# GpSimd's share of the expert chain in halves behind the diagonal, and four kinds of work placed later

## The chip, the cores and the metric

The kernel runs on one core of one Trainium2 chip. The metric is the device time of one execution in microseconds (us). Three runs of the kernel before took 696.67, 700.36 and 705.64 us; the median is 700.36 us. The profiled execution took 699.89 us, of which the profile shows a span of 698.1 us.

## The reference

Four batches of 11456 tokens go through an attention with 49 agents, and the result through a mixture of eight experts of which each token takes one.

```python
def _attn_ref(q, k, v, agents):            # q, k, v: 4 x 11456 x 128, agents: 4 x 49 x 128
    a2k = sm(agents, k)                    # softmax over the tokens
    agent_v = a2k @ v                      # 4 x 49 x 128
    q2a = sm(q, agents)                    # softmax over the 49 agents
    return q2a @ agent_v

def _moe_ref(x, expert_emb, tau, w1, w2):  # x: 45824 x 128, w1: 8 x 128 x 1024, w2: 8 x 1024 x 128
    logits = normed(x) @ normed(expert_emb).T / tau
    expert_idx = argmax(logits); gate_w = softmax(logits)[expert_idx]
    for e in range(8):
        out[mask_e] = gate_w * (relu(x[mask_e] @ w1[e]) @ w2[e])
```

All is float32.

## The kernel before

Per batch `b` the kernel runs over units `u` of eight tokens per partition (and a rest unit): scores of the agents with the keys (`k1_f32`, `k1_pairs`), the product with the values (`k2_unit`), the scores of the queries (`q_unit`), and the expert network over tiles `t` of four tokens per partition (`ffn_mm1`, `ffn_mm2`, `ffn_out`). It assumes that nearly all tokens of a batch take one expert, and prepares that expert's two weight matrices so that only 256 of the 1024 hidden columns have to be worked out for each token; the rest is a linear map (`lin`). Each token is then tested (`proved`, the `vp` products) on whether this was allowed, and the few tokens that fail are marked (`mark_strays`) and done again one by one: `fix(b)` for those of the batch's own expert, `stray` for those of another.

While batch b's network runs, keys, values and queries of batch b+1 are worked through, and near the end of batch b comes what is called **the chain** below: `pick_expert(b+1)`. It loads the expert (`load_expert`: w1s, w2s, one buffer each), forms `gp` = w1 times agent values, from that a sort key for each of the 1024 columns (eight a partition, tiles `mean`, `pw`, `key`: a dozen tiny VectorE instructions, lines 755 to 775), spreads the keys along a diagonal (`diag`, in the tile `sel`, line 772), turns them into one row by a product with ones (`row`, line 784), ranks each column against the row (lines 793 and 795), makes a selection matrix from the ranks (`sel`, line 801), and places the chosen columns (`placed`: gh and gl, the halves of w1; line 809). Then come `linp` (line 842), `w2pp` and its copy `w2p` (lines 856 and 858), the maximum over all partitions that gives the thresholds (`allmax`: a transpose `mT`, a VectorE maximum `mTx`, a product `mB`), a second selection (line 875) and a third `placed`, from which `vm`, the matrix of the tests, is made (line 880). The network of batch b+1 can begin with gh and gl (`hp`, line 1211), its second half needs `w2p` and `lin` (`yp`, lines 1235 to 1249), its tests need `vm`. The chain comes once in the opening (batch 0) and three times under a running network: 0 to 1, 1 to 2 and 2 to 3.

In the chain GpSimd (POOL) has four large instructions: w2s times its scale (line 735) and the remainder of w2 (line 736), the remainder of the placed columns gt (line 790), and diag (line 772, on GpSimd for b > 0).

What sets the order: every engine works through its own list in order. Python generators yield "steps" and so bring the pieces of all stages into one sequence; from that a scheduler makes the list of every engine when the kernel is built, except that the DMA queue of SyncE (SP) keeps the written order. `in_place(y_last)` ties a TensorE instruction behind the last product of the network. Tiles rotate through a few buffers: PSUM has four for `hp`, `fTp` and `vp`, two for `yp` and two for all else (`pss`); a TensorE instruction waits until the engine that reads the old content is done. The transposes of the queries' scores (`tt`, DMA, line 935) go through SP's queue as the key, value, query and expert loads do.

## Time and profile before

| what | value |
|---|---|
| median of three runs | 700.36 us (696.67 to 705.64) |
| profiled execution | 699.89 us, span 698.1 us |
| TensorE busy | 652.2 us, 93% |
| VectorE busy | 535.5 us, 77% |
| ScalarE busy | 453.6 us, 65% |
| GpSimd busy | 355.1 us, 51% |
| mean granted TensorE clock | 0.969 of full speed |

TensorE's two clock levels are 1.2 and 2.4 GHz; the granted clock of a stretch is its mean as a share of the higher. A wait in a view of the trace is idle time of an engine just before an instruction, with the instruction that ended it. An engine that is held up inside an instruction counts as busy: its instruction only lasts longer than others of its form.

### The profile page before, as it was taken

How to read it: one execution, taken by the hardware profiler on the slowest of the kernel's cores; microseconds unless marked ns; L12 is line 12 of the kernel's file. 1: busy time of each engine (PE TensorE's matmuls, PEld its weight loads, DVE VectorE, ACT ScalarE, POOL GpSimd, SP SyncE). 2: the span in 40 equal slices, each digit the busy share in tenths (PEclk: the TensorE clock that was granted, in tenths of full speed). 3: DMA queues.
4: the chain of work that ended last, by engine and by line, in shares of the span. 5: the costliest groups of instructions: out<-in, count | busy, mean ns of one | idle time of the engine just before them, and what ended most of it. 6: DMA issues, size and time to landing. Idle time of an engine off the chain costs nothing. (4 is left out here: it accounts for less than half of the span.)

```text
span 698.1 us, 23174 instructions
## 1 busy us (share of the span) xinstructions
PE 652.2 (93%) x9227; PEld 557.9 (80%) x9227; DVE 535.5 (77%) x1470; ACT 453.6 (65%) x1127; POOL 355.1 (51%) x606
## 2 busy tenths in 40 slices
PE   8998999999998888989999888999999999996996
PEld 6886888888887767878889677888888798775876
DVE  5767796878686988876767888977657889985983
ACT  3538746966887636847688853776577857992632
POOL 6002382675153745873533484685645656876410
PEclk9999999999999989989999997999999999998999
DMA  8995596699692267996959245998575424205141
GB/s 342 281 341 174 133 287 169 144 277 238 204 252 69 62 173 194 303 255 160 256 147 221 83 106 136 267 279 204 151 170 169 113 65 114 59 17 171 54 147 70
DMA packets 157047, 123.16 MB, mean 176 GB/s; under 512 B 76787, under 2 KB 133191, under 8 KB 156939
## 3 DMA queue, kind: packets, MB, share of 16 engines
q1 hardware_dynamic: 143499, 97.97, 55.5%
q10 hardware_dynamic: 13120, 23.47, 9.7%
q8 instruction: 73, 1.20, 0.7%
q14 instruction: 35, 0.29, 0.1%
q0 software_dynamic: 320, 0.24, 0.1%
HBM read 80.26 MB, written 23.79 MB: 149 GB/s over the span
## 5 line engine op out<-in xcount | busy, mean ns | idle before, releaser
L1065 ACT ACTIVATE vp<-vp 128x512 f32<-128x512 f32 x180 | 106.1, 590 | 18.7 <-PE vp L1056 13.1
L1220 ACT ACTIVATE hh<-hp 128x512 f16<-128x512 f32 (+1 forms) x124 | 72.4, 591 | 51.7 <-PE hp L1212 30.7
L438 PE MATMUL sp<-aT_all,fT 128*64 128x49 f32 x2496 | 96.4, 226 | 3.4 <-DVE avx L543 2.0
L1221 DVE SCALAR_TENSOR_TENSOR hh<-hp,hh 128x512 f16<-128x512 f32 (+1 forms) x124 | 82.9, 674 | 21.1 <-ACT hh L1220 18.6
L438 PEld LDWEIGHTS sp<-aT_all,fT 128*64 128x64 f32 x2496 | 84.3, 139 | 16.3 <-issue 3.6
L1247 PE MATMUL yp<-w2p,hh 128*128 128x128 f16 (+1 forms) x492 | 95.0, 223 | 0.1
L1248 PE MATMUL yp<-w2p,hh 128*128 128x128 f16 (+1 forms) x492 | 94.9, 223 | 0.0
L1249 PE MATMUL yp<-w2p,hh 128*128 128x128 f16 (+1 forms) x492 | 93.7, 223 | 0.0
L1056 PE MATMUL vp<-vm,tt 128*128 128x256 f16 x360 | 71.0, 274 | 3.9 <-DVE vmin L1062 2.3
L931 POOL TENSOR_TENSOR e<-qe,e 128x392 f16<-128x392 f32 (+1 forms) x48 | 42.2, 880 | 63.3 <-ACT e L928 62.2
L1211 PE MATMUL hp<-tt,gh 128*128 128x512 f16 (+1 forms) x184 | 69.5, 378 | 3.9 <-DVE hh L1221 1.6
L1263 DVE TENSOR_TENSOR ot<-yp,gs 128x512 f32<-128x512 f32 (+1 forms) x92 | 61.2, 668 | 14.6 <-PE yp L1244 8.7
L430 ACT COPY fT<-fTp 128x512 f32<-128x512 f32 (+1 forms) x103 | 57.0, 569 | 23.6 <-PE fTp L425 19.7
L1006 POOL TENSOR_TENSOR nrm<-qq,half 128x16 f32<-128x16 f32 (+2 forms) x28 | 69.9, 2498 | 0.2
L1212 PE MATMUL hp<-tt,gl 128*128 128x512 f16 (+1 forms) x184 | 69.3, 377 | 0.0
L1235 PE MATMUL yp<-lin,tt 128*128 128x128 f16 x720 | 64.9, 224 | 4.5 <-DVE ot L1263 4.4
L1244 PE MATMUL yp<-w2f,hh 128*128 128x128 f32 (+1 forms) x456 | 66.3, 283 | 0.0
L1244 PEld LDWEIGHTS yp<-w2f,hh 128*128 128x128 f32 (+1 forms) x456 | 60.0, 195 | 4.3 <-issue 0.8
L1235 PEld LDWEIGHTS <-tt 128*128 128x128 f16 x720 | 51.1, 102 | 12.3 <-issue 6.0
L425 PE MATMUL fTp<-ident,qt 128*128 128x128 f32 x360 | 55.0, 284 | 1.2 <-ACT hh L1216 0.9
L1247 PEld LDWEIGHTS <-hh 128*128 128x128 f16 (+1 forms) x492 | 49.4, 100 | 4.4 <-ACT hh L1220 0.3
L963 POOL TENSOR_TENSOR rt<-qe 128x392 f32<-128x392 f32 (+1 forms) x48 | 38.4, 800 | 28.2 <-ACT qe L923 20.1
(371 smaller groups left out, 1713.3 us busy)
## 6 DMA issues: line engine op xcount, KB each, us to landing
kt<-in_k_dram SPq DMA_DIRECT2D x44, 512.0 KB, 5.9
vt<-in_v_dram SPq DMA_DIRECT2D x44, 512.0 KB, 7.3
qt<-in_q_dram SPq DMA_DIRECT2D x44, 512.0 KB, 5.2
out_dram<-ot ACTq DMA_DIRECT2D x88, 256.0 KB, 2.3
w1s<-in_moe_w_dram SPq DMA_DIRECT2D x9, 512.0 KB, 5.2
w2s<-in_moe_w_dram SPq DMA_DIRECT2D x9, 512.0 KB
tt<-e SPq DMA_TRANSPOSE x48, 5.2
kt<-in_k_dram SPq DMA_DIRECT2D x4, 96.0 KB, 3.8
```

Of the source, the lines that this page charges most:

```text
L438: pe.matmul(out=s[h : h + w, c * A : (c + 1) * A], lhsT=xT[:, c * p + h : c * p + h + w], rhs=aT_all[:, b, :], start=True, stop=True, skip ...
L1006: pool.tensor_tensor(out=nrm, in0=quad, in1=half[:, :n], op=ALU.pow)
L1056: pe.matmul(out=z[:p, i * FP : (i + 1) * FP], lhsT=tt[:, c * p : (c + 1) * p], rhs=bt.vm[:, LO:], start=True, stop=True)
L1065: act.activation(z[:p], z[:p], AF.Relu, scale=-1.0, accum_out=bt.vsum[:p, at : at + 1])
L1211: pe.matmul(out=hp[:, :m], lhsT=bt.gh[:, fs], rhs=tt, start=True, stop=False)
L1220: h_last[:] = [act.activation(hh[:, :m], hp[:, :m], AF.Relu)]
L1221: dve.scalar_tensor_tensor(out=hl[:, :m], in0=hp[:, :m], scalar=0.0, in1=hh[:, :m], op0=ALU.max, op1=ALU.subtract)
L1235: pe.matmul(out=yp[:p, c, :], lhsT=tc_, rhs=bt.lin[:, h], start=(c == 0 and h == 0), stop=False, skip_group_check=True)
L1244: y_last[:] = [pe.matmul(out=y, lhsT=hh[:, cs], rhs=bt.w2f[:, f], start=False, stop=last, skip_group_check=True)]
L1247: pe.matmul(out=y, lhsT=hh[:, cs], rhs=wh, start=False, stop=False, skip_group_check=True)
L1248: pe.matmul(out=y, lhsT=hh[:, cs], rhs=wl, start=False, stop=False, skip_group_check=True)
L1249: y_last[:] = [pe.matmul(out=y, lhsT=hl[:, cs], rhs=wh, start=False, stop=last, skip_group_check=True)]
```

## The change

Six things change, all for the chains under a running network (b > 0) if nothing else is said.

- GpSimd's four large instructions are cut into halves, and those of w2s, w2x and gt are tied behind the second half of the diagonal. The two tiny VectorE instructions `nkey` and `sgn` move ahead of the diagonal.
- The VectorE remainder of a key unit (`ks`) is written in two instructions of four tokens instead of one of eight.
- The copy of `w2pp` to `w2p` goes from VectorE to ScalarE.
- The threshold products `mT` and `mB` are asked for some steps later and tied behind the network's last product.
- `mark_strays(b)` goes on when the next batch's `vm` exists, not when its `w2p` does.
- In `fix`, the token gather is asked for first, and for b < 3 the expert load 24 steps after it.

```diff
@@ -208,15 +208,18 @@
             except StopIteration as s:
                 return s.value
 
-    def allmax(col, n, tag, psx, g, bufs=2):
-
+    def allmax(col, n, tag, psx, g, bufs=2, place=None):
+
+        place = place or nullcontext
         t_ = psx("mT")
-        pe.transpose(out=t_[:n, :P], in_=col, identity=ident)
+        with place():
+            pe.transpose(out=t_[:n, :P], in_=col, identity=ident)
         mx = sm.tile([P, 1], F32, name="mTx", tag="mTx")[:n]
         dve.tensor_reduce(out=mx, in_=t_[:n, :P], axis=AX.X, op=ALU.max)
         yield g
         t_ = psx("mB")
-        pe.matmul(out=t_[:, :n], lhsT=mx.broadcast_to([n, P]), rhs=ident[:n, :n], start=True, stop=True)
+        with place():
+            pe.matmul(out=t_[:, :n], lhsT=mx.broadcast_to([n, P]), rhs=ident[:n, :n], start=True, stop=True)
         r = sm.tile([P, n], F32, name="pm", tag=tag, bufs=bufs)
         act.copy(r, t_[:, :n])
         return r
@@ -486,7 +489,9 @@
             pool.tensor_tensor(out=src[:p, :n], in0=src[:p, :n], in1=sc.unsqueeze(2).broadcast_to([p, n, D]), op=ALU.mult)
             pool.tensor_tensor(out=xs[:p, :n, 1], in0=src[:p, :n], in1=xs[:p, :n, 0], op=ALU.subtract)
         else:
-            dve.scalar_tensor_tensor(out=xs[:p, :n, 1], in0=src[:p, :n], scalar=sc, in1=xs[:p, :n, 0], op0=ALU.mult, op1=ALU.subtract)
+            for c in range(0, n, TJ):
+                cs = slice(c, min(c + TJ, n))
+                dve.scalar_tensor_tensor(out=xs[:p, cs, 1], in0=src[:p, cs], scalar=sc, in1=xs[:p, cs, 0], op0=ALU.mult, op1=ALU.subtract)
         used("k", b, u)
         yield 6
         i = yield from take(x_slots)
@@ -732,11 +737,21 @@
             yield g
             act.activation(w2x[:, :, 0], w2s, AF.Copy, scale=s3)
             if b > 0:
-                pool.tensor_tensor(out=w2s, in0=w2s, in1=s3.unsqueeze(2).broadcast_to([P, NF, D]), op=ALU.mult)
-                pool.tensor_tensor(out=w2x[:, :, 1], in0=w2s, in1=w2x[:, :, 0], op=ALU.subtract)
+                for h in halves:
+                    with in_place(made):
+                        pool.tensor_tensor(out=w2s[:, h], in0=w2s[:, h], in1=s3.unsqueeze(2).broadcast_to([P, NF // 2, D]), op=ALU.mult)
+                        pool.tensor_tensor(out=w2x[:, h, 1], in0=w2s[:, h], in1=w2x[:, h, 0], op=ALU.subtract)
             return s3, i3
 
         mean, key, nkey, sgn, pw = col("mean"), col("key"), col("nkey"), col("sgn"), col("pw")
+
+        made = []
+        halves = [slice(0, NF // 2), slice(NF // 2, NF)]
+
+        def signs():
+
+            dve.tensor_scalar(nkey, key, -1.0, None, ALU.mult)
+            dve.tensor_scalar(sgn, mean, 0.0, -0.5, ALU.is_ge, ALU.add)
 
         def order_keys():
 
@@ -769,10 +784,13 @@
             yield 1
             dve.tensor_tensor(out=ki, in0=ki, in1=uid, op=ALU.bitwise_or)
             yield 1
-            vec.tensor_tensor(out=diag, in0=ident.unsqueeze(1).broadcast_to([P, NF, P]),
-                              in1=key.unsqueeze(2).broadcast_to([P, NF, P]), op=ALU.mult)
-            dve.tensor_scalar(nkey, key, -1.0, None, ALU.mult)
-            dve.tensor_scalar(sgn, mean, 0.0, -0.5, ALU.is_ge, ALU.add)
+            if b > 0:
+                signs()
+            for h in halves:
+                made[:] = [vec.tensor_tensor(out=diag[:, h], in0=ident.unsqueeze(1).broadcast_to([P, NF // 2, P]),
+                                             in1=key[:, h].unsqueeze(2).broadcast_to([P, NF // 2, P]), op=ALU.mult)]
+            if b == 0:
+                signs()
 
         i2 = yield from (beside(order_keys(), first_scale()) if b == 0 else beside(first_scale(), order_keys()))
         if b > 0:
@@ -787,7 +805,10 @@
             act.copy(row[:, hs], t_)
             yield g
 
-        pool.tensor_tensor(out=gs_[1], in0=gg, in1=gs_[0], op=ALU.subtract)
+        for h in halves:
+            with in_place(made) if b > 0 else nullcontext():
+                pool.tensor_tensor(out=gs_[1][:, 2 * h.start : 2 * h.stop], in0=gg[:, 2 * h.start : 2 * h.stop],
+                                   in1=gs_[0][:, 2 * h.start : 2 * h.stop], op=ALU.subtract)
         rank, more = col("rank"), col("more")
         for c in range(NF // 2):
             dve.tensor_scalar(junk[0], row, key[:, c : c + 1], 0.0, ALU.is_lt, ALU.add, accum_out=rank[:, c : c + 1])
@@ -855,7 +876,7 @@
                 for c in range(NF):
                     pe.matmul(out=t_[:, k_ * 2 * D : (k_ + 1) * 2 * D], lhsT=sel[:, c, (f + k_) * P : (f + k_ + 1) * P],
                               rhs=w2x[:, c].rearrange("p h d -> p (h d)"), start=(c == 0), stop=(c == NF - 1))
-            (act.copy if f % 4 else dve.tensor_copy)(w2p[:, f : f + nk].rearrange("p f h d -> p (f h d)"), t_[:, : nk * 2 * D])
+            (act.copy if b > 0 else dve.tensor_copy)(w2p[:, f : f + nk].rearrange("p f h d -> p (f h d)"), t_[:, : nk * 2 * D])
             yield g
         bt.w2p = w2p
         iall = sm.tile([P, 1], F32, name="iall", tag="iall")
@@ -865,7 +886,8 @@
         bt.iall = iall
         dve.tensor_scalar(rank, rank, -float(FM), None, ALU.add)
         yield 1
-        top = yield from allmax(gmx, 2, "gmxr", psx, 1)
+        yield 2 * g
+        top = yield from allmax(gmx, 2, "gmxr", psx, 1 + 3 * g, 2, lambda: in_place(y_last if b > 0 else []))
         thr = sm.tile([P, 1], F32, name="thr", tag="thr")
         bt.far = sm.tile([P, 1], F32, name="far", tag="far")
         dve.tensor_scalar(thr, top[:, :1], 1.05 * 2.0 ** -11, None, ALU.mult)
@@ -1086,7 +1108,7 @@
         idx = sm.tile([P, NCOL], F32, name="idx", tag="idx", bufs=1)
         dve.tensor_reduce(out=idx, in_=oh, axis=AX.X, op=ALU.min)
         yield 1
-        while b < B - 1 and not hasattr(batches[b + 1], "w2p"):
+        while b < B - 1 and not hasattr(batches[b + 1], "vm"):
             yield 1
         odd = sm.tile([P, NCOL], F32, name="odd", tag="odd", bufs=1)
         ne = sm.tile([P, NCOL], F32, name="ne", tag="ne", bufs=1)
@@ -1376,9 +1398,10 @@
         dve.tensor_scalar(none, bt.fix[:, :1], 0.5, 2 * BIG, ALU.is_lt, ALU.mult)
         yield 1
         dve.scalar_tensor_tensor(out=ix, in0=bt.fix[:, :1], scalar=-1.0, in1=none, op0=ALU.add, op1=ALU.add)
+        xq = gather(ix)
+        yield 24 if b < B - 1 else 0
         w1s, w2s = load_expert(bt.e0i)
-        xq = gather(ix)
-        yield 24 if b < B - 1 else 8
+        yield 0 if b < B - 1 else 8
         yield from answer(xq, ix, bt.fix[:, 1:], aT_all[:, b], av_all[:, b], w1s, w2s, (b + 1) * NT)
         bt.fixed = True
 
```

What the change moves on the engines, at three places. The first is GpSimd's list in the chain 0 to 1, before (e is the scores' remainder of a query unit, rt the squares of one):

```order
L1027 TENSOR_TENSOR el<-el,la 128x16
L931 TENSOR_TENSOR e_0_149<-qe,e_0_149 128x8x49
L735 TENSOR_TENSOR w2s<-w2s,hsc 128x1024
L967 TENSOR_TENSOR rt<-rt 128x16x24
L790 TENSOR_TENSOR gt_152<-gts,gt_152 128x16x49
L772 TENSOR_TENSOR sel<-ident,key 128x1024
L736 TENSOR_TENSOR w1s<-w2s,w1s 128x8x128
L963 TENSOR_TENSOR rt<-qe 96x98
```

and now (lines of the changed file: 790 is the diagonal, 742 and 743 are w2s and w2x, 810 is gt):

```order
L1049 TENSOR_TENSOR el<-el,la 128x16
L953 TENSOR_TENSOR e_0_149<-qe,e_0_149 128x8x49
L989 TENSOR_TENSOR rt<-rt 128x16x24
L790 TENSOR_TENSOR sel<-ident,key 128x512 x2
L742 TENSOR_TENSOR w2s<-w2s,hsc 128x512 x2
L810 TENSOR_TENSOR gt_152<-gts,gt_152 128x8x49 x2
L985 TENSOR_TENSOR rt<-qe 96x98
L743 TENSOR_TENSOR w1s<-w2s,w1s 128x4x128 x2
```

The diagonal stood behind w2s and gt and stands now ahead of both.

The second place is the end of the chain 1 to 2. TensorE's list around the threshold products, before:

```order
L856 MATMUL w2pp<-w1s,sel 128x256
L214 MATMUL mT<-ident,gmx 2x128
L1211 LDWEIGHTS gh
L1211 MATMUL hp<-tt,gh 128x512
L1212 LDWEIGHTS gl
L1212 MATMUL hp<-tt,gl 128x512
L219 MATMUL mB<-ident,mTx 128x2
L438 MATMUL sp<-aT_all,fT 64x49 x16
```

and now around `mB` (line 222 of the changed file; 1269 to 1271 are the network's products with w2p, 1233 and 1234 those of hp):

```order
L1271 LDWEIGHTS hh
L1271 MATMUL yp<-w2p,hh 128x128
L1233 LDWEIGHTS gh
L1233 MATMUL hp<-tt,gh 128x512
L1234 LDWEIGHTS gl
L1234 MATMUL hp<-tt,gl 128x512
L222 MATMUL mB<-ident,mTx 128x2
L1269 LDWEIGHTS hh
L1269 MATMUL yp<-w2p,hh 128x128
```

Between `mT` and `mB` stood one pair of hp; now twelve lin products and four w2f products of network tiles, sixteen score products, two pairs of hp and twelve products with w2p stand there. VectorE's list at the same place, before (sp is a query unit's scores, qmx and qe read it; gate_all, odd, ne, idx and lga belong to the marks):

```order
L1082 TENSOR_SCALAR lga<-lga 128x720
L1093 TENSOR_SCALAR odd<-vmin 128x90
L918 TENSOR_REDUCE qmx<-sp 128x8
L1106 TENSOR_SCALAR gate_all<-esa 128x90
L969 TENSOR_REDUCE qq<-rt 128x2x8
L1099 SCALAR_TENSOR_TENSOR odd<-vsum,odd 128x90
L921 TENSOR_TENSOR qe<-sp,qmx 128x392
L1108 RECIPROCAL gate_all<-gate_all 128x90
L1103 TENSOR_TENSOR odd<-odd,ne 128x90
```

and now (940 and 943 are qmx and qe, 1104 to 1130 the marks):

```order
L940 TENSOR_REDUCE qmx<-sp 128x8
L1045 TENSOR_REDUCE esa<-ex 128x10
L1104 TENSOR_SCALAR lga<-lga 128x720
L1115 TENSOR_SCALAR odd<-vmin 128x90
L991 TENSOR_REDUCE qq<-rt 128x2x8
L943 TENSOR_TENSOR qe<-sp,qmx 128x392
L1128 TENSOR_SCALAR gate_all<-esa 128x90
L1121 SCALAR_TENSOR_TENSOR odd<-vsum,odd 128x90
L1052 RECIPROCAL gs<-el 128x10
L867 SCALAR_TENSOR_TENSOR lin<-linp,lin 128x128
L1130 RECIPROCAL gate_all<-gate_all 128x90
L1125 TENSOR_TENSOR odd<-odd,ne 128x90
```

The marks still stand here, ahead of the second selection and of `vm`; but `qe` is now ahead of `gate_all`.

The third place is SP's queue near the end, where the last query units of batch 3 are transposed (tt) and `fix(2)` loads its expert. Before:

```order
L935 DMA_TRANSPOSE tt<-e_1_150 128x8x128
L885 TENSOR_LOAD e0i
L885 ISA x2
L888 ISA
L888 DMA w1s<-in_moe_w_dram 128x1024
L889 ISA
L889 DMA w2s<-in_moe_w_dram 128x8x128
L935 DMA_TRANSPOSE tt<-e_0_149 128x8x128
L935 DMA_TRANSPOSE tt<-e_1_150 128x2x96
```

and now:

```order
L957 DMA_TRANSPOSE tt<-e_1_150 128x8x128
L957 DMA_TRANSPOSE tt<-e_0_149 128x8x128
L957 DMA_TRANSPOSE tt<-e_1_150 128x2x96
L907 TENSOR_LOAD e0i
L907 ISA x2
L910 ISA
L910 DMA w1s<-in_moe_w_dram 128x1024
L911 ISA
L911 DMA w2s<-in_moe_w_dram 128x8x128
```

The two last transposes now go ahead of the load. The loads of `fix(0)` and `fix(1)` stand nine and eight transfers later in the queue than before.

## Rows read from the trace of the kernel before

**Rows 1.** The page: busy time by engine, and TensorE's granted clock in 40 slices.
```profile
PE 652.2 (93%) x9227; PEld 557.9 (80%) x9227; DVE 535.5 (77%) x1470; ACT 453.6 (65%) x1127; POOL 355.1 (51%) x606
PEclk9999999999999989989999997999999999998999
```

**Rows 2.** TensorE's waits: us in total, times, longest.
```profile
PE mB L219 <- DVE mTx L216: 3.6, 3, 2.5
PE vp L1056 <- DVE vmin L1062: 2.3, 1, 2.3
PE w2pp L856 <- DVE qe L921: 2.0, 1, 2.0
```

**Rows 3.** Stretches of 10 us: busy time by engine, granted clock, DMA share, GB/s.
```profile
210.00:220.00 10.00, 8.81 (x54) 7.17 (x54) 4.64 (x11) 5.02 (x13) 4.71 (x4) 0.83 0.23 85
...
240.00:250.00 10.00, 6.66 (x93) 5.40 (x92) 10.00 (x27) 2.47 (x7) 7.45 (x17) 0.95 0.38 72
250.00:260.00 10.00, 9.80 (x128) 8.00 (x129) 7.30 (x33) 3.47 (x10) 2.27 (x7) 0.71 0.73 221
...
410.00:420.00 10.00, 6.68 (x45) 4.79 (x43) 9.48 (x23) 3.70 (x10) 8.30 (x17) 0.81 0.53 117
420.00:430.00 10.00, 8.75 (x112) 7.24 (x113) 8.83 (x37) 2.94 (x8) 2.11 (x10) 0.68 0.75 181
...
630.00:640.00 10.00, 4.20 (x58) 3.66 (x58) 4.40 (x10) 1.00 (x4) 8.64 (x12) 0.73 0.77 227
```

**Rows 4.** Timeline of GpSimd, chain 0 to 1: start us, us, instruction.
```profile
205.74 1.90 POOL L735 TENSOR_TENSOR w2s<-w2s,hsc 128x1024 f32<-128x1024 f32 x1 [2.79 <-ACT w1s L733]
...
208.41 1.69 POOL L790 TENSOR_TENSOR gt<-gts,gt 128x784 f16<-128x784 f32 x1
210.42 1.90 POOL L772 TENSOR_TENSOR sel<-ident,key 128x1024 f32<-128x1024 f32 x1 [0.31 <-DVE key L770]
```

**Rows 5.** Timeline of VectorE in the same stretch.
```profile
206.18 1.48 DVE L765 SCALAR_TENSOR_TENSOR key<-key,mean 128x8 f32<-128x8 f32 x1
...
208.52 1.62 DVE L768 TENSOR_SCALAR key<-key 128x8 int32<-128x8 int32 x1
...
210.45 0.68 DVE L1062 TENSOR_REDUCE vmin<-vp 128x8 f32<-128x512 f32 x1
```

**Rows 6.** Timeline of TensorE at four places.
```profile
217.91 1.88 PE L784 MATMUL row<-sel,ones 128*128 128x512 f32 x4
...
232.39 1.91 PE L809 MATMUL placed<-sel,gt 128*128 128x256 f16 x16
...
248.05 0.38 PE L1211 MATMUL hp<-tt,gh 128*128 128x512 f16 x1 [1.48 <-DVE fT L428]
...
386.06 0.61 PE L1235 MATMUL yp<-lin,tt 128*128 128x128 f16 x8 [2.17 <-DVE ot L1263]
...
636.24 0.23 PE L946 MATMUL rtp<-r_hi,tt 128*128 128x58 f16 x1 [4.28 <-DMA tt<-e]
```

**Rows 7.** Timeline of VectorE, chain 1 to 2.
```profile
383.81 1.60 DVE L774 TENSOR_SCALAR nkey<-key 128x8 f32<-128x8 f32 x1
...
412.27 1.66 DVE L1106 TENSOR_SCALAR gate_all<-esa 128x90 f32<-128x90 f32 x1
...
420.06 0.68 DVE L858 CAST w2p<-w2pp 128x512 f16<-128x512 f32 x1
```

**Rows 8.** Timeline of SP's DMA queue near the end.
```profile
628.21 0.35 SPq L888 DMA_DIRECT2D w1s<-in_moe_w_dram  x1
630.58 0.38 SPq L889 DMA_DIRECT2D w2s<-in_moe_w_dram  x1
631.01 4.69 SPq L935 DMA_TRANSPOSE tt<-e  x2
```

**Rows 9.** Timeline of GpSimd: what the waiting transpose reads.
```profile
626.23 0.91 POOL L931 TENSOR_TENSOR e<-qe,e 128x392 f16<-128x392 f32 x1 [0.62 <-POOL rtg L124]
```

**Rows 10.** The groups by line: the key units' remainder on VectorE.
```profile
L489 DVE SCALAR_TENSOR_TENSOR ks<-kt,hsc,ks 128x1024 f16<-128x1024 f32 x12 | 17.1, 1427 | 6.9 <-ACT ks L483 6.7
```

## The prediction

> **What bounds the kernel now.** I began with the page's busy times and clock row [rows 1]. TensorE is busy 652.2 of 698.1 us, and the granted clock is below 90% of full speed in four of 40 slices. So there are 45.9 us of TensorE idleness to win, and what the clock takes. VectorE follows with 77%. Only the places matter where TensorE waits. TensorE's list comes out the same in both programs in its opening, and nearly so up to the first chain under a running network, so nothing changes before 200 us.
>
> Then TensorE's waits [rows 2], to see who ends them. The wait of `mB`, that of a test product `vp` and that of `w2pp` are all ended by VectorE. TensorE is fed late there by an engine that is itself late.
>
> Then the stretches of 10 us [rows 3], to see where idleness and slow clock fall together. They do so at the chains and near the end: 210 to 220, 240 to 260, 410 to 430 and 630 to 640. In these six stretches TensorE is busy 8.81, 6.66, 9.80, 6.68, 8.75 and 4.20 us, so 15.1 of 60 us are idle. What the clock takes I reckon as busy time times the missing share of the clock: 1.5, 0.3, 2.8, 1.3, 2.8 and 1.1 us, 9.8 us in all.
>
> Last the timelines, to see why VectorE is late. In the chain 0 to 1 GpSimd runs w2s from 205.74 to 207.64, gt from 208.41 to 210.10 and the diagonal from 210.42 [rows 4]. Two VectorE instructions on eight columns last 1.48 and 1.62 us, and their ends, 207.66 and 210.14, are the ends of w2s and gt to within 0.04 us [rows 5]. So GpSimd's long instructions hold VectorE's tiny ones. Behind these stands `vmin` at 210.45, a reduction out of PSUM, which lasts its 0.68 us although the diagonal is running. It is the one for which the `vp` product waits 2.3 us [rows 2, 5].
>
> **The change part by part.** All sums are against the profiled execution, 699.9 us, 0.5 us below the median of 700.4.
>
> *Diagonal first, chain 0 to 1.* w2s and gt go behind the diagonal, so the key instructions lose the two holds of 1.48 and 1.62 us, down to the 0.2 us or so that such an instruction lasts otherwise: 2.7 us sooner. `vmin` then comes at about 207.8, and the `vp` product loses its wait: 2.3 us [rows 2, 5]. Bounds: 0 (rt, which stays in front, holds them instead) to 2.3. I take 2.3, since `vmin` is needed only at 208.9 (the wait's end less its length).
>
> *Diagonal first, chain 1 to 2.* There `nkey` lasts 1.60 us beside the diagonal [rows 7], the network's output `ot` stands behind it, and TensorE waits 2.17 us for `ot` [rows 6]. `nkey` now stands ahead of the diagonal: 2.2 us gained; bounds 0 to 2.2.
>
> *Halves.* The cut itself moves no data. Half of an instruction of 1.90 us is 0.95 us [rows 4], so a VectorE instruction caught by it is held for at most that long. It has a price on GpSimd, some tenths per cut at most, and this is covered, since GpSimd is busy 51% [rows 1].
>
> *w2p to ScalarE.* VectorE loses an instruction of 0.68 us that began only at 420.06, behind the second selection [rows 7]. ScalarE is busy 3.70 and 2.94 of 10 us in these stretches [rows 3], which covers the copy. The products with w2p can start some 2 us sooner.
>
> *Threshold products later.* At the end of the chain 1 to 2 `mB` waits 2.5 us with the whole network queued behind it [rows 2]. Now two pairs of hp and 28 yp products stand in front of it, which is more work than the wait lasted. I take 2.5 us; bounds 0 to 2.5. `vm` comes later, and only the tests wait for it, whose buffers are not the network's outputs.
>
> *w2pp.* Its 2.0 us wait [rows 2] is for `qe`, ahead of which stood a mark's `gate_all` of 1.66 us [rows 7]. `qe` is now in front of that, but two other marks stay in front of `qe`. I take 1.0; bounds 0 to 2.0.
>
> *The same in the chain 0 to 1.* The stretch from 240 has 3.3 us of idleness [rows 3], of which 1.48 us is one pair of hp behind VectorE's copy `fT` [rows 6], and `mB`'s shorter wait is in it too. VectorE gives up `w2p` here as well, so `fT` comes earlier. I take 2.0; bounds 0 to 3.3.
>
> *Marks later.* As the lists stand, most of the marks' VectorE instructions still lie ahead of the second selection. I take nothing for this part.
>
> *Expert loads later.* Near the end SP's queue stood at the load until w1s could be overwritten: w1s went at 628.21, w2s at 630.58, and only then the transposes at 631.01 [rows 8]. What the first one reads was done at 627.14 [rows 9]. It landed by 636.24, where TensorE had waited 4.28 us [rows 6]. Now both transposes go first: 3.9 us sooner by these rows, and by more since the scores they come from stand earlier in TensorE's list. I take 4.3; bounds 3.0 to 4.3. The load of `fix(2)` comes some 7 us later, and its first use stands behind a gather, two products and a softmax. `fix(0)` and `fix(1)` load nine and eight transfers later, ahead of the same steps.
>
> *ks in two.* Twelve instructions of 1.43 us [rows 10] become 24. Their own price lies between nothing and as much again, 17.1 us of VectorE over the whole run; the nearest row is the uncut instruction, one pass over the same 1024 elements, so I put it near nothing.
>
> *What is late next.* In the chain 0 to 1 the second half of `row` moves earlier by some 1.5 us of TensorE work and the first `placed` by 4. The time between their starts, 14.5 us [rows 6], was filled by the ranks on VectorE, so `placed` can now wait for them. Bounds 0 to 4; I charge 2.
>
> *Clock.* Each slow stretch lies at or right behind a wait that goes or shrinks [rows 3]. Of the 9.8 us I take half, 4.9; bounds 0 to 9.8.
>
> The sum: 2.3 + 2.2 + 2.5 + 1.0 + 2.0 + 4.3 + 4.9 - 2.0 = 17.2 us. I don't believe all of it. VectorE is busy 10.00, 9.48 and 8.83 of 10 us in the stretches from 240, 410 and 420 [rows 3], so TensorE cannot gain more there than VectorE can follow: I take 3 us back. The lists of all engines come out newly sorted around each chain and in the last fifth, and each such stretch can hold a new wait like those of 1 to 2 us that are there now: another 3 us. That leaves 11.2 us: 699.9 - 11.2 = 688.7, so **689 us**, 1.6% below the median.
>
> **A rule against the change.** The rows show VectorE held to the end of a GpSimd instruction [rows 4, 5]; cutting GpSimd's work helps there. But `ks` itself reads two tiles in SBUF and lasts 1.43 us in the mean [rows 10]. The Trainium skill (SBUF — State Buffer, "Who interferes with whom") says that a VectorE instruction with two SBUF inputs and a GpSimd instruction that reads SBUF exclude each other for a whole instruction, whichever began first. By that rule the cut of `ks` gives GpSimd an opening in the middle of it. The trace agrees with the hold (1.62 us instead of some 0.2); none of its rows shows a cut `ks`.
>
> **The rivals.**
>
> 1. *VectorE gives it back.* The waits of `mB` and `vp` go and come again at other VectorE results, since VectorE is full at 240 and 410 [rows 3]. For it: every wait of rows 2 is VectorE's. Against it: the end's 4.3 us is a DMA's and is not touched by this. What remains is 4.3 us and that stretch's clock, 1.1, less the charge of 2: 699.9 - 4.3 - 1.1 + 2.0 = 696.5, or 697 us.
>
> 2. *Slower: GpSimd in the middle of `ks`.* A half of 0.95 us [rows 4] gets between the two parts in all twelve key units [rows 10]: 11.4 us more for VectorE. It decides the time where VectorE has no slack, which is the chains 1 to 2 and 2 to 3 and the stretch behind each. If all of it reaches TensorE and, of the gains, only the end's and the first `vp` wait's stay, 4.3 + 2.3: 699.9 + 11.4 - 6.6 = 705 us. Against it: only in the chains are GpSimd's instructions dense, and TensorE waits for a `ks` only through VectorE's queue.
>
> 3. *The clock stays up.* All 9.8 us come back and nothing is given back: 699.9 - 17.2 - 4.9 = 678 us. For it: in the stretches that are not named, with TensorE busy throughout, the clock is at 90% or more [rows 1]. Against it: the waits shrink but don't vanish.
>
> 4. *It does not do what it says.* This holds for the marks already, and if the diagonal's lead were lost to rt as well, 2.3 + 2.2 us go: 693 us. This lies inside the range.
>
> **How the numbers follow.** My forecast, 684 to 695 with rival 4, has a chance of 0.56; rival 1 (695 to 701) 0.20; rival 2 (701 to 712) 0.12; rival 3 (676 to 684) 0.12. The range that leaves out about 0.1 on each side is 679 to 702. A change of 2% is 14.0 us (the three runs shown lie within 1.3%), that is below 686.4 or above 714.4. Faster by more: all of rival 3 and some 0.14 of the forecast's 0.56, 0.26. Slower by more: the tail of rival 2, 0.03. Within 2%: 0.71.
>
> **What would show it.** Right: no wait of 2 us of a `vp` for `vmin` near 209; key instructions of 0.2 us in all chains; `mB` with no wait above 0.5 us; no wait for `tt` near 630; fewer half-speed stretches. Wrong: waits of 1 us or more for `placed`, `linp` or `hp` ended by VectorE, or `ks` halves with gaps between them (rivals 1 and 2). If the time is above 700 with these waits gone, the step that failed is the one from a wait removed to time gained.

## The result, and the profile after

The changed kernel takes 679.7 us (median of four runs, 675.8 to 682.5), the kernel before 698.5 in the same session: a ratio of 0.971 with a 95% interval of 0.962 to 0.980. It is faster by 18.8 us, where 689 and "within 2%" were forecast. Here and below a ratio leaves out the runs that took over 1.5% longer than the fastest of their kernel. The profiled executions are 699.9 and 679.8 us; all readings below are between these two, spans 698.1 and 677.9.

The page first: busy time by engine and the granted clock in 40 slices. Against [rows 1], TensorE's idle time fell from 45.9 to 34.4 us, by 11.5, and its busy time by 8.7 with the same 9227 products, which is the clock's share for the most part. VectorE's busy time fell by 12.8.
```profile
PE 643.5 (95%) x9227; PEld 552.0 (81%) x9227; DVE 522.7 (77%) x1480; ACT 453.4 (67%) x1130; POOL 354.6 (52%) x619
PEclk9997999999999979989999999999999999999999
```
TensorE's waits (us in total, times, longest), the three of [rows 2]:
```profile
PE mB L222 <- DVE mTx L218: 1.8, 2, 1.4
PE vp L1078 <- DVE vmin L1084: 1.1, 2, 0.6
PE w2pp L877 <- DVE w1s L870: 1.1, 1, 1.1
```
The 2.3 of `vp`, the 2.0 of `w2pp` for `qe` and the 2.5 of `mB` in the chain 1 to 2 are gone (the `w2pp` that is left belongs to the opening). The `mB` of 1.4 is the one of the chain 0 to 1, where it was 0.73. Other waits are new or longer; three places in TensorE's timeline, the first beside the 1.48 of [rows 6], the others without a counterpart at their place before:
```profile
244.37 0.38 PE L1233 MATMUL hp<-tt,gh 128*128 128x512 f16 x1 [1.65 <-DVE fT L431]
...
408.62 0.38 PE L1257 MATMUL yp<-lin,tt 128*96 128x128 f16 x4 [1.86 <-DVE ot L1285]
...
619.53 0.38 PE L1233 MATMUL hp<-tt,gh 128*128 128x512 f16 x1 [1.89 <-DVE hh L1243]
```

Stretches of 10 us (busy time by engine, granted clock, DMA share, GB/s), those that answer to [rows 3]; the places lie 2 us later near 210, 3 earlier near 250, 12 earlier near 410 and some 18 earlier near 630:
```profile
210.00:220.00 10.00, 10.00 (x121) 8.21 (x121) 7.39 (x15) 9.23 (x22) 8.69 (x9) 1.00 0.47 128
240.00:250.00 10.00, 6.66 (x101) 5.10 (x98) 9.52 (x27) 3.34 (x10) 6.07 (x17) 0.79 0.53 133
250.00:260.00 10.00, 10.00 (x149) 8.90 (x148) 8.37 (x32) 4.04 (x9) 5.48 (x11) 0.87 0.82 169
400.00:410.00 10.00, 8.14 (x99) 7.18 (x98) 9.99 (x24) 3.72 (x11) 9.38 (x18) 1.00 0.51 127
410.00:420.00 10.00, 10.00 (x174) 8.35 (x173) 10.00 (x40) 4.88 (x13) 3.56 (x14) 1.00 0.79 177
610.00:620.00 10.00, 8.11 (x106) 6.48 (x104) 5.80 (x14) 6.42 (x23) 6.83 (x13) 1.00 0.30 87
```
The stretch from 240 has as little work as before, 6.66 us, and the two from 240 are still partly at the half clock (0.79 and 0.87). In the other four the clock is full. TensorE works 8.14 and 10.00 us from 400 to 420, against 6.68 and 8.75 from 410 to 430 before, although VectorE is busy 9.99 and 10.00 there.

VectorE and GpSimd in the chain 0 to 1, against [rows 4, 5] (start us, us, instruction):
```profile
208.55 0.87 DVE L782 TENSOR_SCALAR key<-key 128x8 f32<-128x8 f32 x1
209.45 0.17 DVE L783 TENSOR_SCALAR key<-key 128x8 int32<-128x8 int32 x1
209.86 0.17 DVE L753 TENSOR_SCALAR nkey<-key 128x8 f32<-128x8 f32 x1
209.94 0.69 DVE L1084 TENSOR_REDUCE vmin<-vp 128x8 f32<-128x512 f32 x1
```
```profile
208.52 0.87 POOL L989 TENSOR_TENSOR rt<-rt 128x384 f32<-128x384 f32 x1 [3.39 <-DVE key L780]
209.97 2.04 POOL L790 TENSOR_TENSOR sel<-ident,key 128x512 f32<-128x512 f32 x2 [0.58 <-DVE key L785]
```
The two holds of 1.48 and 1.62 us are gone; one of 0.87 is left, and it ends with `rt` (209.39 and 209.42), the instruction that stayed in front. The diagonal begins only when the last key is through, and `nkey`, which stands ahead of it now, is not held. In the chain 1 to 2 it is the same: `nkey`, 1.60 us in [rows 7], lasts 0.17.
```profile
376.32 0.17 DVE L753 TENSOR_SCALAR nkey<-key 128x8 f32<-128x8 f32 x1
376.41 0.69 DVE L1285 TENSOR_TENSOR ot<-yp,gs 128x512 f32<-128x512 f32 x1
```
The cut `ks` against [rows 10]: 1.1 us more for VectorE in the whole run.
```profile
L494 DVE SCALAR_TENSOR_TENSOR ks<-kt,hsc,ks 128x512 f16<-128x512 f32 x24 | 18.2, 798 | 1.8 <-ACT ks L486 1.7
```
Near the end SP issues the last transposes without the load between them, against [rows 8]:
```profile
589.56 35.43 SPq L957 DMA_TRANSPOSE tt<-e  x4
625.82 0.36 SPq L910 DMA_DIRECT2D w1s<-in_moe_w_dram  x1
```

Where the 20.2 us lie shows when the starts of the same `hp` product are set side by side (both timelines hold 184 rows of `hp` with `gh`):

| `hp` row | before | after | gained so far | stage that ends there, gain |
|---|---|---|---|---|
| 1 | 85.22 | 87.40 | -2.2 | opening, -2.2 |
| 61 | 293.31 | 290.59 | 2.7 | chain 0 to 1, 4.9 |
| 73 | 347.63 | 341.52 | 6.1 | stretch near 300, 3.4 |
| 85 | 386.95 | 380.81 | 6.1 | 0 |
| 103 | 451.18 | 436.60 | 14.6 | chain 1 to 2, 8.4 |
| 133 | 551.68 | 537.18 | 14.5 | chain 2 to 3, 0 |
| 181 | 678.60 | 657.68 | 20.9 | last 140 us, 6.4 |
| span | 698.1 | 677.9 | 20.2 | tail, -0.7 |

The stages are less sure than the total. Row i of `hp` does not stand beside the same other work in both lists: row 157 alone would show 6.3 and row 163 shows 18.8. And equal lists differ in time too. The kernel before and the same kernel with a later scatter (the last experiments) have the same lists on TensorE, VectorE, ScalarE and GpSimd up to 600 us, yet from row 1 to row 73 the second takes 5.5 us less, 2.7 of it between rows 61 and 73. The stretch from 300 in these two:
```profile
300.00:310.00 10.00, 9.64 (x98) 8.08 (x96) 6.43 (x15) 4.16 (x12) 7.55 (x12) 0.66 0.92 255
```
```profile
300.00:310.00 10.00, 9.19 (x131) 7.94 (x131) 7.95 (x20) 5.37 (x15) 9.11 (x14) 1.00 1.27 287
```
So a single stage is sure to some us only, and the 3.4 us of the stretch near 300 need not come from the change.

### The profile page after: what moved, and what is told of

Its sections match the earlier page's. It is cut to its first block, busy times and chain, and to the rows that moved or that the text cites. A ratio compares the mean times of both kernels' runs of the same rounds, so it can differ in the third digit from the quotient of the medians.

```text
span 677.9 us, 23199 instructions
## 1 busy us (share of the span) xinstructions
PE 643.5 (95%) x9227; PEld 552.0 (81%) x9227; DVE 522.7 (77%) x1480; ACT 453.4 (67%) x1130; POOL 354.6 (52%) x619
## 5 line engine op out<-in xcount | busy, mean ns | idle before, releaser
L441 PE MATMUL sp<-aT_all,fT 128*64 128x49 f32 x2496 | 98.1, 228 | 1.3 <-DVE m_run L413 0.7
L1243 DVE SCALAR_TENSOR_TENSOR hh<-hp,hh 128x512 f16<-128x512 f32 (+1 forms) x124 | 83.1, 675 | 19.5 <-ACT hh L1242 18.9
L441 PEld LDWEIGHTS sp<-aT_all,fT 128*64 128x64 f32 x2496 | 86.0, 141 | 14.0 <-issue 4.5
L1270 PE MATMUL yp<-w2p,hh 128*128 128x128 f16 (+1 forms) x492 | 93.2, 220 | 0.0
L1269 PE MATMUL yp<-w2p,hh 128*128 128x128 f16 (+1 forms) x492 | 93.1, 220 | 0.0
L1271 PE MATMUL yp<-w2p,hh 128*128 128x128 f16 (+1 forms) x492 | 92.0, 220 | 0.4 <-DVE hh L1243 0.4
L1028 POOL TENSOR_TENSOR nrm<-qq,half 128x16 f32<-128x16 f32 (+2 forms) x28 | 68.2, 2436 | 0.3
L1257 PE MATMUL yp<-lin,tt 128*128 128x128 f16 x720 | 63.0, 222 | 4.5 <-DVE ot L1285 4.5
L1266 PE MATMUL yp<-w2f,hh 128*128 128x128 f32 (+1 forms) x456 | 63.8, 280 | 0.0
L1266 PEld LDWEIGHTS yp<-w2f,hh 128*128 128x128 f32 (+1 forms) x456 | 57.9, 192 | 3.0 <-issue 0.5
L1257 PEld LDWEIGHTS <-tt 128*128 128x128 f16 x720 | 49.2, 100 | 12.1 <-issue 6.5
L989 POOL TENSOR_TENSOR rt<-rt 128x384 f32<-128x384 f32 (+1 forms) x48 | 41.2, 858 | 24.7 <-DVE rt L986 17.1
```

The costliest lines, as they stand in the source:

```text
L441: pe.matmul(out=s[h : h + w, c * A : (c + 1) * A], lhsT=xT[:, c * p + h : c * p + h + w], rhs=aT_all[:, b, :], start=True, stop=True, skip ...
L1243: dve.scalar_tensor_tensor(out=hl[:, :m], in0=hp[:, :m], scalar=0.0, in1=hh[:, :m], op0=ALU.max, op1=ALU.subtract)
L1257: pe.matmul(out=yp[:p, c, :], lhsT=tc_, rhs=bt.lin[:, h], start=(c == 0 and h == 0), stop=False, skip_group_check=True)
L1266: y_last[:] = [pe.matmul(out=y, lhsT=hh[:, cs], rhs=bt.w2f[:, f], start=False, stop=last, skip_group_check=True)]
L1269: pe.matmul(out=y, lhsT=hh[:, cs], rhs=wh, start=False, stop=False, skip_group_check=True)
L1270: pe.matmul(out=y, lhsT=hh[:, cs], rhs=wl, start=False, stop=False, skip_group_check=True)
```

## The experiments

All ratios are to the kernel before, run on the same chip in the same session; there it had medians of 697.7 to 698.8. The parts undone are compared below with 679.8 us, the median of the kernel with the marks undone, whose lists are those of the changed kernel, also where they ran in another session.

| kernel | median us | ratio, 95% interval | TensorE's wait beside the stray's answer, us | longest stretch of its list there without a `yp` |
|---|---|---|---|---|
| before | 698 | 1 | 4.28 + 1.50 | 79 |
| changed | 679.7 | 0.971, 0.962 to 0.980 | 1.89 | 39 |
| marks undone | 679.75 | 0.973, 0.969 to 0.977 | 1.84 | 39 |
| loads undone | 684.9 | 0.981, 0.977 to 0.985 | 0.90 | 33 |
| chain undone | 683.6 | 0.977, 0.972 to 0.982 | 0.86 | 33 |
| thresholds undone | 689.5 | 0.987, 0.983 to 0.992 | 4.11 | 63 |
| w2p undone | 690.4 | 0.990, 0.983 to 0.996 | 3.81 | 83 |
| ks undone | 679.8 | 0.976, 0.970 to 0.983 | 1.52 | 31 |
| whole, ordered | 678.4 | 0.972, 0.966 to 0.978 | 1.48 | 33 |
| loads alone | 699.7 | 1.000, 0.997 to 1.004 | 4.23 | 59 |
| chain alone | 688.6 | 0.986, 0.980 to 0.992 | 2.50 + 1.50 | 65 |
| thresholds alone | 696.2 | 0.998, 0.994 to 1.002 | 3.35 + 1.64 | 55 |
| w2p alone | 704.5 | 1.010, 1.004 to 1.017 | 2.28 + 1.99 | 59 |
| thresholds and w2p | 691.1 | 0.989, 0.983 to 0.995 | 0.98 | 33 |

The stray's answer is the repair by the function `stray`; it ends, with a scatter of the repaired rows into the output, near 631 us before and 614 after. The last column is counted in the instruction lists, in products from one `yp` to the next, within 300 products of the answer's last `syp`.

### Each part undone in the changed kernel

Theory A takes the prediction's terms without its deductions, B lets the clock's dips come by chance, C lets VectorE's busy time decide; D came up after the first results.

Loads (the old order of `fix`):
```diff
-        xq = gather(ix)
-        yield 24 if b < B - 1 else 0
         w1s, w2s = load_expert(bt.e0i)
-        yield 0 if b < B - 1 else 8
+        xq = gather(ix)
+        yield 24 if b < B - 1 else 8
```


> The changed kernel with one part undone: the expert loads of the three repairs stand again ahead of the gather. Theory A (each wait that went reaches the end whole and takes a stretch of half clock with it): the 4.28 us wait of TensorE for tt near the end comes back, with the 1.5 us wait of yp behind it and 1.5 to 3 us of half-speed clock; 6 to 9 us longer than the changed kernel, so 686 to 689 where that one has 680. Theory B (the waits gave what they lasted, and the clock's stretches come and go by chance): 4.3 us longer, 684. Theory C (what gave the time is VectorE's relief, 12.8 us less busy time; the transfers at the end would have been covered): 0 to 1 us.

5.1 us longer (684.9 against 679.8), but not where A has it. SP's queue near the end is held again, w1s until 611.67 and w2s until 615.29, and the transposes go 3.3 us after the scores are there (612.52). TensorE waits 0.90 us for them. SP's queue and the wait:
```profile
611.67 0.35 SPq L910 DMA_DIRECT2D w1s<-in_moe_w_dram  x1
615.29 0.38 SPq L911 DMA_DIRECT2D w2s<-in_moe_w_dram  x1
615.78 12.24 SPq L957 DMA_TRANSPOSE tt<-e  x2
```
```profile
621.33 0.20 PE L968 MATMUL rtp<-r_hi,tt 128*128 128x58 f16 x1 [0.90 <-DMA tt<-e]
```
By the `hp` rows 3.8 us of it arise between rows 103 and 109, where the load of `fix(1)` stands (437.10) and `tt` is waited for 0.98 and 2.21 us, and 2.4 between rows 175 and 181, 650 to 664 us. B's total was hit for another reason.

Marks:
```diff
-        while b < B - 1 and not hasattr(batches[b + 1], "vm"):
+        while b < B - 1 and not hasattr(batches[b + 1], "w2p"):
```


> The changed kernel with one part undone: the marks wait for the next batch's second weights again instead of for its vm. The instruction lists of all engines come out word for word as in the changed kernel, so this is also a second run of it. All theories: no difference (680 within 0.5%). Theory A: its stretches of half-speed clock lie where the changed kernel's did, behind the same waits. Theory B: the stretches that don't follow a wait of a microsecond, above all the one at 54.6 us in the unchanged opening, move or are absent, and with them 1 to 3 us.

No difference, as every theory had it: the part does nothing to the lists. As a second execution of one program it shows what a profile carries by chance: the two agree within 1.1 us at every `hp` up to the stretch of 240, and the 6.8 us of half clock behind 54 us are in both. That was theory B's test, and this pair doesn't bear B out; the pair at 300 us above and the openings in the last section do.

Chain (the four GpSimd pieces and the signs as in the kernel before):
```diff
-                for h in halves:
-                    with in_place(made): ...
+                pool.tensor_tensor(out=w2s, ...)
+                pool.tensor_tensor(out=w2x[:, :, 1], ...)
-            if b > 0:
-                signs()
             ... diag ...
+            signs()
```


> The changed kernel with one part undone: GpSimd's chain work whole again and not ordered, nkey and sgn behind the diagonal. Theory A: key instructions of 1 to 4 us come back on VectorE, TensorE's two waits near 211 and 386 (2.26 and 2.17 us) too, with 1.5 to 3 us of half-speed clock at 211: 6 to 8 us longer, 686 to 688. Theory B: 4.4 us longer, 684.5. Theory C: VectorE's busy time returns to some 532 us and all chains and the 300 us stretch lose: 10 us or more, 690 or above.

3.8 us longer, with intervals of the ratio that overlap. The holds are back (`nkey` up to 1.64 us, the key's mask 1.62), and so is the first wait, but of the second, 2.17 us near 386, only 0.96 near 375, and VectorE's busy time is 529 us. TensorE at the first wait:
```profile
212.55 0.60 PE L1078 MATMUL vp<-vm,tt 128*128 128x256 f16 x4 [2.27 <-DVE vmin L1084]
```
C's mechanism is refuted by the size; A's total was too large by 2 to 4 us.

Thresholds:
```diff
-        yield 2 * g
-        top = yield from allmax(gmx, 2, "gmxr", psx, 1 + 3 * g, 2, lambda: in_place(y_last if b > 0 else []))
+        top = yield from allmax(gmx, 2, "gmxr", psx, 1)
```


> The changed kernel with one part undone: the threshold products at their old place in all chains. Theory A: a wait of mB of 2 to 2.5 us at the end of chain 1 to 2 comes back, with half-speed clock behind it worth 1 to 3 us: 4 to 5 us longer, 684 to 685. Theory B: 2.5 us, 682.5. Theory C: VectorE does the same work either way: 0 to 1 us.

9.7 us longer, twice what A had. `mB` waits 4.05 us in the chain 1 to 2, and a wait that no theory had comes at the end:
```profile
410.81 0.35 PE L222 MATMUL mB<-ident,mTx 2*128 2x2 f32 x2 [4.05 <-DVE mTx L218]
...
625.57 1.01 PE L1257 MATMUL yp<-lin,tt 128*128 128x128 f16 x8 [4.11 <-DVE ot L1285]
```

w2p, ks, and the halving:
```diff
-            (act.copy if b > 0 else dve.tensor_copy)(w2p[...], t_[...])
+            (act.copy if f % 4 else dve.tensor_copy)(w2p[...], t_[...])
```


> The changed kernel with one part undone: two of the eight copies of w2p per chain on VectorE again. Theory A: fT in chain 0 to 1 and the copies behind the second selections come 0.7 us later, 1 to 2 us longer: 681 to 682. Theory D: the lists come out anew, so 0 to 6 us longer, most of it behind 560 us.

10.6 us longer, against 1 to 2 by A and at most 6 by D, which had the place right. (A chain has one copy of `w2p`, 0.68 us on VectorE as in [rows 7], not eight; the edit puts back one in each of three chains.) In the chain 1 to 2 a score product now waits for that copy, and the wait at the end is there again:
```profile
413.99 1.14 PE L441 MATMUL sp<-aT_all,fT 128*64 128x49 f32 x32 [1.86 <-DVE w2p L879]
...
629.06 1.01 PE L1257 MATMUL yp<-lin,tt 128*128 128x128 f16 x8 [3.81 <-DVE ot L1285]
```
```diff
-            for c in range(0, n, TJ):
-                cs = slice(c, min(c + TJ, n))
-                dve.scalar_tensor_tensor(out=xs[:p, cs, 1], ...)
+            dve.scalar_tensor_tensor(out=xs[:p, :n, 1], ...)
```


> The changed kernel with one part undone: ks in one piece. Theory A (the cut costs VectorE about 1 us in all and moves nothing): 680 within 1.5 us, VectorE 521 to 523 us busy. Rival 2 of the prediction (GpSimd in the middle of ks): shorter than the changed kernel, down to 669. Theory D (every edit sorts the lists anew in the last fifth, and there waits of 1 to 4 us come and go whatever was edited): up to 6 us longer, with a new wait of over 1 us behind 560 us and none of them near a ks.

No difference in time (679.8), though VectorE is busy 527.5 us and not 521 to 523: rival 2 of the prediction had no ground, and the cut of `ks` is worth nothing that the runs can tell. D fails here.
```diff
-                for h in halves:
-                    with in_place(made): ... w2s[:, h] ...
+                with in_place(made): ... w2s ...
```


> The changed kernel with GpSimd's chain instructions whole again, but ordered as in the change (nkey and sgn first, then the diagonal, then w2s and gt). Theory A (the order does it, the halving nothing): key instructions stay at 0.2 us, no 2.3 us wait of vp near 211, 680 to 681. Theory H (the halving does it): nkey or another VectorE instruction is held for 1.5 us or more beside a whole GpSimd instruction, and the time goes back to that of the undone chain, 683 to 684.

678.4 us, and the keys are as short as in the changed kernel (`nkey` at most 0.17 us in the four chains) beside a diagonal of 1.90 us in one piece. The order does it; the halving does nothing that these runs can tell. This kernel has the lowest median of all, but its interval and that of the changed one overlap.

### Parts alone on the kernel before

> The kernel before with one part of the change alone: gather first, expert loads later. Theory A (SP's queue held the transposes near the end, as the prediction's term has it): the 4.28 us wait for tt near 636 goes, with the 1.5 us behind it and the half-speed stretch at 634: 6 to 9 us less, 689 to 692 where the kernel before has 698. Theory B (from the undone load, where the hold of SP's queue came back but TensorE waited only 0.9 us near the end: how far ahead of their use the scores stand in TensorE's list decides, and the load order counts only at the second repair, near 450): a wait of 2 us or more for tt or for ot stays near 636, 0 to 3 us less, 695 to 698.

699.7: nothing gained. The hold of SP's queue is gone (no load between the transposes), and TensorE stands still at the same place, now for `ot`. SP's queue, GpSimd, ScalarE's DMA queue, VectorE and TensorE:
```profile
605.95 35.23 SPq L935 DMA_TRANSPOSE tt<-e  x5
642.83 0.36 SPq L888 DMA_DIRECT2D w1s<-in_moe_w_dram  x1
```
```profile
637.20 1.11 POOL L1365 DMA_INDIRECT out_dram<-so,ix  x1 [0.70 <-DVE rmx L1002]
```
```profile
639.46 4.14 ACTq L1269 DMA_DIRECT2D out_dram<-ot  x5
```
```profile
618.18 0.68 DVE L1263 TENSOR_TENSOR ot<-yp,gs 128x512 f32<-128x512 f32 x1
...
641.53 0.69 DVE L1263 TENSOR_TENSOR ot<-yp,gs 128x512 f32<-128x512 f32 x1 [1.03 <-DMA out_dram<-ot]
```
```profile
642.28 1.01 PE L1235 MATMUL yp<-lin,tt 128*128 128x128 f16 x8 [4.23 <-DVE ot L1263]
```
All three buffers of `ot` were full by 618.86, the first by 605.25, but no store left between 598.62 and 639.46. ScalarE's list has other work ahead of the next store until 638.79, and the store goes 2.3 us after GpSimd issued the stray's scatter into the same output (637.20). That this scatter holds ScalarE is named in the waits of other runs: 2.05 us with w2p alone, 2.44 in the changed kernel (its line stands below, with the later scatter). The kernel before shows the same: three `ot` by 613.19, the scatter issued at 631.23, the first store at 635.89. So the stall comes without the cause that the prediction named.

> The kernel before with GpSimd's chain part alone: halves behind the diagonal, nkey and sgn ahead of it. Theory L: the waits at 211 and 386 go (2.3 and 2.2 us) with the half-speed stretch at 211; the list still has the stretch of twelve pairs without yp, so the end's wait stays: 692 to 695. Theory P: the same.

688.6, 9.1 us less than the kernel before in the session (697.7) and more than either theory had. Besides the two waits at 211 and 386, those of `w2pp` and `mB` in the chain 1 to 2, 2.0 and 2.5 us, are gone too, without a threshold product moved; 1.13 and 1.76 us for `ot` and `w2p` stand there instead. TensorE's waits of the chain:
```profile
414.59 0.38 PE L1250 MATMUL yp<-lin,tt 128*96 128x128 f16 x4 [1.13 <-DVE ot L1278]
418.52 0.22 PE L1262 MATMUL yp<-w2p,hh 128*128 128x128 f16 x1 [1.76 <-DVE w2p L873]
```


> The kernel before with the threshold products later, and nothing else. Theory L: the list still has the stretch of ten pairs without yp, so the end's wait of some 4 us stays; only mB's 2.5 us wait at 421 goes, with some of the half-speed clock behind it: 693 to 696. Theory P: the same. Were the threshold products alone the cause of the 9.7 us that undoing them cost, it would be 688 to 690.

696.2, no difference that the interval shows; the wait at the end is there, as L had it. The 2.5 us wait of `mB` is gone, and a score product waits 1.91 us for `w2p` at 418 instead.

> The kernel before with all of w2p on ScalarE, and nothing else. Theory L: the list still has the stretch of ten pairs without yp, so the end's wait stays; 0 to 2 us less in the chains: 696 to 698. Were w2p alone the cause of the 10.6 us that undoing it cost, it would be 687 to 689.

704.5, slower by 1%, which nobody expected. The wait at the end stays, and two more come behind it, for the marks of the last batch:
```profile
667.59 0.27 PE L1162 MATMUL mine<-mparts,mput 128*128 128x6 f16 x5 [2.75 <-POOL mparts L1155]
670.11 0.40 PE L214 MATMUL mT<-ident,cnt_p 128*32 128x128 f32 x1 [2.26 <-DVE cnt_p L1190]
```
By the `hp` rows 6.9 us are lost between rows 175 and 181. Why this program's list has these waits and the others' don't was not tried.

> The kernel before with two parts of the change alone: threshold products later, and all of w2p on ScalarE. Expert loads, chain order and halves stay as before. Theory L (near the end TensorE stands still where its list has a stretch of ten pairs of hp with no yp between them, beside the stray repair's scatter; in this program's list the longest such stretch has two): no wait of 3 us or more between 600 and 640; the two parts give their 3 to 5 us in the chains and the end's 8 to 10 us besides, so 684 to 687. Theory P (the prediction's term: the loads' hold of SP's queue makes the end's wait): the wait of 4 us for tt or ot stays, 693 to 695.

691.1: together the two give 6.6 us, where alone they give 1.5 and -6.8. The end has no wait above 0.98 us, with the loads where they were, so P is refuted for the end; L's total was too low by 4 to 7 us, since the first `vp` wait (2.28 us) and others in the chains stay.

### The scatter behind the last store

In `stray`, the last step is left to a generator that waits for all output stores; the result lies in a tile that is dead by then, and its row numbers in one of their own (those lines are left out below):
```diff
-        while len(stored) < tiles:
-            yield 1
-        pool.indirect_dma_start(out=out, ...)
+        if last:
+            spawn(scatter(o, ix, B * NT))
+        else:
+            yield from scatter(o, ix, tiles)
```


> The kernel before with gather first and loads later (the run that changed nothing), and in addition the scatter of the stray repair moved behind the last output store; its result tile takes the place of a tile that is dead by then. Theory S (near the end the scatter into the output holds the output stores behind it, those hold ot's buffers, and TensorE stands still because no test products are left in its list there; the load's hold and the scatter's hold are two causes of one stall, so that taking away one gives nothing): the 4.2 us wait of yp for ot near 642 goes, with half-speed clock of up to 3 us: 689 to 693. Theory Q (the stall comes from somewhere else, or from how the lists come out): 697 to 700.

> The kernel before, with the scatter of the stray repair behind the last output store and nothing else. Theory S: the load's hold of SP's queue is still there, so the wait for tt near 636 stays at 2 to 4 us and only the 1.5 us wait for ot behind it goes: 694 to 698. Theory Q: 698. If it falls to 692 or below, the scatter alone was the cause and the load none.

> The changed kernel with two copies of w2p per chain on VectorE again (690 us), and the scatter of the stray repair behind the last output store. Theory S: the 3.8 us wait of yp for ot near 629 and its half-speed clock go: 681 to 684; what stays of the 10.6 us is w2p's own price in the chains, 1 to 3 us. Theory Q: 688 to 691.

> The changed kernel with the scatter of the stray repair behind the last output store. Theory S: its stores are held there too (ScalarE stands 2.4 us behind one), but TensorE has test products to do; only the 1.9 us wait of hp at 619 goes: 677 to 679. Theory Q: 680.

At the place S is right in all four: no wait of over 1 us for `tt` or `ot` is left there, and in the list no stretch without a `yp` is longer than 38 products. Against the same program with the early scatter, the lead grows between `hp` rows 157 and 163 by 7.1 us with the loads alone (from 5.9 to 13.1) and by 6.4 with w2p undone (from 3.4 to 9.7). ScalarE's DMA queue and the stretch of 10 us with the loads alone; with the early scatter this stretch read 7.53 us of TensorE, and the next 7.72 at a clock of 0.66:
```profile
625.55 0.34 ACTq L1269 DMA_DIRECT2D out_dram<-ot  x1
632.92 0.34 ACTq L1269 DMA_DIRECT2D out_dram<-ot  x1
635.52 0.34 ACTq L1269 DMA_DIRECT2D out_dram<-ot  x1
```
```profile
630.00:640.00 10.00, 9.81 (x165) 8.71 (x161) 7.56 (x18) 4.99 (x16) 7.02 (x10) 1.00 0.17 59
```
In the total S was right for the kernel before alone. The medians are 696.3, 697.1, 684.4 and 682.2 us, ratios 1.000 (0.996 to 1.003), 0.998 (0.995 to 1.002), 0.984 (0.978 to 0.990) and 0.978 (0.972 to 0.983). Only the third has a clearly lower median than its early form (690.4), and even there the ranges overlap (683.2 to 690.4 and 687.5 to 694.5). What I had not counted is the tail, in which the two last scatters now wait for each other. From `hp` row 181 to the end it takes 24.5 us with the loads alone, against 19.5 before, and 22.5 in the changed kernel, against 20.2. GpSimd there, loads alone:
```profile
684.24 1.03 POOL L1372 DMA_INDIRECT out_dram<-so,ix  x1 [14.24 <-DVE so L1362]
687.50 0.99 POOL L1372 DMA_INDIRECT out_dram<-so,ix  x1 [2.22 <-DMA out_dram<-so,ix]
```
With the kernel before, S expected the 2 to 4 us wait for `tt` to stay. It went, although SP's queue was held until 628.89: so there, too, the load did not set the end. The changed kernel has the scatter's hold still, but work beside it; ScalarE there:
```profile
617.98 0.28 ACT L945 ACTIVATE qe<-qe 96x98 f32<-96x98 f32 x1 [2.44 <-DMA out_dram<-so,ix]
```

## Why the prediction was wrong, point by point

**The failed step: "I don't believe all of it".** The sum stood at 17.2 us; the two deductions of 3 us, for a full VectorE and for newly sorted lists, took the forecast from 682.7 to 688.7. Without them the terms for waits make 12.3 us, with them 6.3; TensorE's idle time fell by 11.5 between the two profiles. The first deduction has no row of the result behind it: in the chain 1 to 2, with VectorE full from 400 to 420, TensorE gained 8.4 us all the same. I read this as a wait not for VectorE's throughput but for a result that stood behind held or early instructions. The second has some: the waits of 1.86 and 1.89 us at 408.62 and 619.53 are new. But they cost less than what else was gained. A term was mis-sized as well: for the clock I took 4.9 us, and TensorE's busy time fell by 8.7. With the whole sum the forecast would have missed by 3 us. Newly sorted lists do move the time, by +6.8 us with w2p alone, but in this change their largest effect, at the end, was a gain: most of what the thresholds and w2p cost when undone lies there.

**Stage by stage** the sum was near, in part by luck, since the stages are sure to some us only and terms that were wrong made up for each other: chain 0 to 1 predicted 2.3 + 2.0 - 2.0 + 2.3 (half of 4.6 us of clock) = 4.6, the trace has 4.9; chain 1 to 2 predicted 2.2 + 2.5 + 1.0 + 2.05 = 7.75, the trace 8.4; end 4.3 + 0.55 = 4.85, the trace 5.7 with the tail. The stretch near 300, where I priced nothing, gave 3.4: the 2.0 us wait of `sp` for `avx` at 299 became 1.4 of `sqT`, and the half-speed stretch there was halved, which chance alone can do, as the pair at 300 shows. The prediction's list of slow stretches left this one out: it is one of the four slices below 90% in [rows 1], and at 9.64 us and 0.66 the clock takes 3.3 us there. The opening took 2.2, by no part of the change.

**The terms behind these sums were less right than they.**
- *Diagonal first, 0 to 1*: right, 2.26 us and the half-speed stretch behind it; undone, 2.27 is back. *1 to 2*: right that `nkey` is freed. But the same lateness of VectorE was also what `w2pp` and `mB` waited for: the chain part alone takes all four waits away. The threshold products alone take `mB`'s, and with the chain part in but not they, `mB` waits 4.05 us. So 2.2, 1.0 and 2.5 were not three gains to be added.
- *Threshold products* and *w2p*: alone 1.5 us and a loss; undone 9.7 and 10.6. No term of mine could have these sizes, since most of it lies at the end, where I saw no link to them.
- *The same in the chain 0 to 1* (2.0) did not come: `fT` 1.65 us and `mB` 1.43 stand where 1.48 and 0.73 stood, 6.66 us busy from 240 as before. It was made up by the charge of 2.0 for `placed`, which did not come either.
- *Expert loads* (4.3): wrong as a cause at the end. Done alone it gives nothing, and the end is free of the wait in two programs with the loads still early (thresholds and w2p; late scatter). The wait of 4.28 us ended with a transpose that SP had held, and I took the last releaser for the only one. The scatter's hold on the stores stood behind it. What the loads are worth in the changed kernel, 5.1 us, lies elsewhere.
- *Clock*: half of 9.8 us taken; four of the six stretches have it whole again and the two from 240 still miss 6.66 x 0.21 + 10.00 x 0.13 = 2.7 us, so 7.1 came back in these. *Marks*: nothing, as predicted. *ks, halves*: nothing, as predicted.

**The signs.** Of those named as right, the `vp` wait near 209 and the wait for `tt` near 630 are gone and half-speed stretches fewer; but two keys are still held (0.87 and 0.84 us), and `mB` waits 1.43. Of those named as wrong, waits of `hp` for VectorE of 1 us or more are there (1.65 and 1.89; 1.48 and 1.41 before), in a kernel faster than forecast. So these signs did not tell the cases apart. The row named beside the rule on two inputs, 1.62 us, is of an instruction with one; the one with two is the 1.48.

**The rivals.** 1 did not come. 2 was refuted directly (ks undone, no difference). 3, at 678, is what the time looks like, and nothing taken back was right; but all of the clock back holds only in part: there is still half clock at 246 and 297. The chance of 0.12 for it was too low, as the deductions had no better ground than it.

**What is shown and what is argued.** Shown: the order and not the halving frees the keys; thresholds and w2p together, not the loads, free the end; the early scatter is needed for the stall there, as moving it alone ends the stall in three programs, in one of them with the load still early. That TensorE's lists lack a `yp` there because the order is made up with the stores held is argued from the lists, which have the gap with the early scatter and not with the late one; why thresholds and w2p close it as well was not found. What the parts give does not add up: alone -9.1 (chain), -1.5 (thresholds), +6.8 (w2p) and +0.9 (loads), in sum -2.9, together -18.8 (`ks` and the marks were not tried alone; undone they change nothing).

## What to carry to other kernels

Waits that one late engine ends are one account: price the lateness once, by stage, and see what else would end the same wait before a term is put down to the last releaser. A deduction needs a row as much as a gain does; without one it belongs in the range, not in the forecast. In a kernel whose order is made by a planner, undo each part in the new version and do each alone in the old one before naming a cause: here the part that was worth 10.6 us by the one made the kernel slower by the other.
